# Token mixing whose result is made already transposed: one half of one batch in PSUM, the other half by DMA

## Chip, cores and metric

The kernel runs on one core of a Trainium2 chip. The metric is the device time of one execution in microseconds (us), as the median of several runs. The chip's profiler gives, for one execution, what each engine did: TensorE (PE, with its weight loads as PEld), VectorE (DVE), ScalarE (ACT), GpSimd (POOL) and SyncE (SP), whose queue issues most of the DMAs.

## What is computed

A gated linear recurrence over 768 tokens, in 4 batches with 8 heads of 48, gives x of 768 x 384 for each batch; a token and channel mixer follows.

```python
for t in range(S):                                   # B, H, S, D = 4, 8, 768, 48
    state = alpha[:, :, t, :, None] * state + k_t (outer) v_t
    y[:, :, t] = q_t @ state
x = y as (B, S, H * D)                               # 768 tokens x 384 channels
h = relu(x^T @ w_tok1) @ w_tok2                      # 768 -> 256 -> 768, over the tokens
u = x + h^T
out = u + relu(u @ w_ch1) @ w_ch2                    # 384 -> 1536 -> 384, over the channels
```

Inputs, weights and output are float32; the products are made in bfloat16 with float32 sums.

## The kernel before

**Pieces.** A batch is cut into three attention blocks of 256 tokens, numbered 0 to 11 over the four batches (0, 1, 2 are batch 0's). For each block four loads of 384 KB bring alpha, k, q and v (`ld_at`, `ld_kt`, `ld_qt`, `ld_vt`). ScalarE takes logarithms, TensorE sums them up (`cum`, or `cumw` in batch 0), ScalarE makes the factors `E` and `IE`, VectorE or GpSimd scale k and q by them (`kk`, `qq`; line 700), TensorE or the DMA transposes them (`trk`, `trq`; line 712; `dk`, `dq`; line 725), a copy brings them to SBUF (`evk`, `evq`), TensorE makes the scores (`G0`, `G1`), VectorE masks them (`mask`, line 770), and TensorE makes the state (`K`) and the output (`ia`, `ib`, `y`), which is copied to x (`x0`, `x1`: two tiles of 128 tokens to a block). The state is carried on with one addition and one multiplication (`sa` line 841, `sm` line 844). `vs`, `ka`, `kb` and `kc` are copies that shift halves between partitions.

**Mixer.** `t1_b_m_kc` (line 878) sums x^T @ w_tok1 over the six token tiles, `ht` is its relu (lines 873 and 875). `t2_b_i` (line 883) makes the tile of 128 tokens with number i of h^T, by two products of 384 columns, and `u_b_i` (line 887, VectorE) adds x and writes u in bfloat16. The channel products need u^T. For batch 0 (`UP = (0,)`) TensorE transposes u in 18 products of 128 columns (`up`, line 894), and three copies of 768 columns bring the result to `ut`; for the other batches the DMA transposes u in two halves of three tiles each (`ux`, line 729, issued by SP). `c1_b_mc_half` (line 902) makes hidden columns 128 mc to 128 mc + 127 for the first or the second three token tiles in three products of 384 columns; `rt` is its relu. `c2_b_i_q4` (line 907) sums the second channel product for token tile i in four parts of three products, `o` (line 911, VectorE) adds u, and `st` stores 192 KB. The last token tile to be done, tile 0 of batch 3, is cut into two column halves, `h0` and `h1`.

**Weights.** Each weight piece is loaded as 384 KB of float32 into one of the 19 buffers `in` (`ldw`) and cast into its bfloat16 place (`cw`). A piece of w_ch1 is one of three chunks of 128 input channels by 768 hidden columns; a `c1` waits for three pieces (0, 1, 2 for mc under 6, else 3, 4, 5). A piece of w_tok2 is one of two chunks of 128 rows by all 768 tokens; each `t2` waits for both.

**Order.** The program names every operation in one list, `ORDER`, whose last letter says the engine: t TensorE, s ScalarE, v VectorE, g GpSimd, y SP. Every engine works through its own operations in that order, and waits in it. `BUFS` gives the buffer of each value in the same order. So what runs beside what, and what stands behind a wait, can be read from the list. Operations of VectorE and GpSimd that share a port (`kk`, `qq`, `vb`, `vs`, `ka`, `kb`, `kc`, `sm`, `P`, `k0a`, `q0r`, `pq`, `cw`) wait for each other wherever the list changes from the one engine to the other. `f1_...` to `f12_...` are filler products of 512 columns on zeros: the number is how many such units they are worth, and the rest of the name is the operation ahead of which they stand. PSUM has eight banks; `pair` values take two adjacent ones.

The list of before around the place of the change begins batch 0's mixer with `t1_0_0_0t f1_G0_2t G0_2t`, goes on to

```
t1_0_1_4t x1_2s t1_0_0_4t f1_t1_0_1_5t t1_0_1_5t ht_0_1v P4g cw_wt21s t1_0_0_5t ht_0_0s f3_t2_0_0t t2_0_0t t2_0_1t
```

and, after the token products, has `cum4t trk3t ut_0_0v up_0_2t ut_0_2v ut_0_1s c1_0_11_0t c1_0_8_0t` among the loads and scalings of block 3.

Of the kernel before, what the change touches and what calls it, by code (L numbers as in the profile page):

```python
# [9 lines left out]
BF16 = mybir.dt.bfloat16  # L10
# [84 lines left out]
B, H, S, D = 4, 8, 768, 48  # L95
# [6 lines left out]
UP = (0,)  # L102
# [18 lines left out]
def build(g):  # L121

    P = Plan()
# [6 lines left out]
    def fillers():  # L130
        for o in list(P.ops):
            nm = o.name
            if "PE" in o.eng and (nm[:4] in ("t1_0", "t2_0", "up_0") or nm.split("_")[-1][-1] in "0123" and nm[:2] not in ("t1", "t2", "up", "c1", "c2") and not nm.endswith("10") and not nm.endswith("11")):
# [182 lines left out]
    def mixer(b):  # L316
# [15 lines left out]
        us = []  # L332
        for i in range(NS):
            if i % 3 == 0:
                u = V("u")
            bank = V("one")
            o = P.op(f"t2_{b}_{i}", pe([384] * 2), m0 + (1900 + 330 * i) * sc, writes=[bank],
                     reads=[h for h, _ in hts], preds=[h for _, h in hts] + [wl[("wt2", p)] for p in range(2)],
                     emit=lambda e, i=i, bank=bank: g.tok2(bank, i, [h for h, _ in hts]))
            uo = P.op(f"u_{b}_{i}", dve(384), m0 + (1950 + 330 * i) * sc, writes=[u], reads=[bank, x[i][0]], preds=[o],  # L340
                      emit=lambda e, i=i, bank=bank, u=u: g.uadd(u, i, bank, x[i][0]))
            us.append((u, uo))
        ut = V("ut")
        uts = []
        if b in UP:
            for p in range(3):
                bank = V("one")
                o = P.op(f"up_{b}_{p}", pe([128] * 6), m0 + (3900 + 340 * p) * sc, writes=[bank],
                         reads=list(dict.fromkeys([us[2 * p][0], us[2 * p + 1][0]])),
                         preds=[us[2 * p][1], us[2 * p + 1][1]],  # L350
                         emit=lambda e, p=p, bank=bank: g.utr(bank, [us[2 * p][0], us[2 * p + 1][0]], p))
                uts.append(P.op(f"ut_{b}_{p}", either(dve(768, True), act(768)), m0 + (3950 + 340 * p) * sc, writes=[ut],
                                reads=[bank], preds=[o], emit=lambda e, p=p, bank=bank: g.utev(e, ut, bank, p)))
        else:
            for half in range(2):
                uts.append(P.op(f"ux_{b}_{half}", {"SP": (1240.0, 1240.0)}, m0 + (3900 + 500 * half) * sc, writes=[ut],
                                reads=[us[3 * half][0]], preds=[us[3 * half + i][1] for i in range(3)],
                                emit=lambda e, half=half: g.uxbar(ut, us[3 * half][0], half),
                                dma=("x", 1450.0, 1180.0, 480.0)))
# [13 lines left out]
        for i in range(NS):  # L373
            hold = 4000.0 if (i >= NS - 3 and b < B - 1) else 0.0
            cuts = [(0, HD // 2), (HD // 2, HD)] if (b, i) == LAST else [(0, HD)]
            for ci, (ca, cz) in enumerate(cuts):
# [3 lines left out]
                for q4 in range(4):  # L380
                    pp = []
                    for mc in range(3 * q4, 3 * q4 + 3):
                        pp.append(rts[mc][1][i // 3])
                    prev = P.op(f"c2_{nm}_{q4}", pe([cz - ca] * 3), m0 + (16700 + 1950 * i + 487 * q4) * sc + hold,
                                writes=[bank], reads=[rts[mc][0] for mc in range(3 * q4, 3 * q4 + 3)],
                                preds=pp + [wl[("wc2", mc // 2)] for mc in range(3 * q4, 3 * q4 + 3, 2)] + ([prev] if prev else []),
                                emit=lambda e, i=i, q4=q4, bank=bank, ca=ca, cz=cz: g.ch2(bank, i, q4, rts, ca, cz))
                oo = P.op(f"o_{nm}", dve(cz - ca), m0 + (16750 + 1950 * (i + 1)) * sc + hold, writes=[o_],
                          reads=[bank, us[i][0]], preds=[prev],
                          emit=lambda e, i=i, bank=bank, o_=o_, ca=ca, cz=cz: g.oadd(o_, bank, us[i][0], i, ca, cz))  # L390
# [19 lines left out]
ld_at1y ld_at0y ln1s ln0s f8_cumw1t f1_cumw1t cumw1t IE1s cumw0t IE0s ld_vt0y E0s vb0g vs0_0g vs1_0v ld_kt0y kk0v  # L410
f8_trk0t f1_trk0t trk0t E1s ld_qt0y qq0v ka0s kb0s kc0v f1_trq0t trq0t ld_kt1y kk1v K0t evq0s s0_0v ld_vt1y vb1s
f1_trk1t trk1t ld_at2y evk0v ln2s f2_G0_0t G0_0t ld_qt1y ka1g sa1_0v f4_cumw2t cumw2t mask0_0v vs0_1s kb1g kc1g vs1_1s
K1t sm1_0g qq1v sa0_1v sm0_1v G1_0t ld_kt2y IE2s E2s trq1t evq1s ib0t mask1_0v f3_y1_0t y1_0t y0_0t evk1v G0_1t sa1_1v
ld_qt2y x1_0s mask0_1v G1_1t ld_vt2y x0_0s vb2s kk2g trk2t kc2s ldw_wt10y qq2g cw_wt10s f2_ia1t ia1t mask1_1v evk2s
trq2t ld_at3y vs1_2g ldw_wt11y evq2v ib1t y1_1t y0_1t vs0_2g ldw_wt21y sm1_1g P3g K2t sa0_2v sm0_2g x0_1s t1_0_0_0t
f1_G0_2t G0_2t ldw_wt20y G1_2t cw_wt20g t1_0_1_0t mask0_2v x1_1s t1_0_1_1t ld_at4y ld_kt3y t1_0_1_2t lnP3s cum3t
# [549 lines left out]
```

## Time and profile before

| | before |
|---|---|
| median of 3 runs (lowest, highest) | 163.35 us (163.22, 163.51) |
| span of the profiled execution, from its first to its last instruction | 160.5 us |
| own time of the profiled execution | not on the page; it has the span alone |
| TensorE busy | 154.6 us, 96% of the span |
| VectorE busy | 114.9 us, 72% |
| ScalarE busy | 97.8 us, 61% |
| GpSimd busy | 80.8 us, 50% |
| granted TensorE clock | 1.000 |
| DMA traffic | 35.05 MB, mean 218 GB/s |

A row of the timeline gives start, length, engine, line, operation and the tiles out<-in. A row of groups gives the count, the busy time and the mean duration of one, and the idle time of the engine ahead of them with what ended it. Matmuls are pipelined, so the durations of neighbours overlap; the spacing of a long run of them tells the price of one. "SPq" is SP's queue at the issue of a DMA. A table by stretches gives for each stretch the busy time of each engine, the granted clock, the DMA share and GB/s.

### The profile page before, as it was taken

The numbers are of one execution on the slowest core, as the hardware profiler recorded it, in microseconds if no ns is written. First come the engines' busy times: TensorE is split into PE (matmuls) and PEld (weight loads), VectorE is DVE, ScalarE is ACT, GpSimd is POOL, SyncE is SP. The second block draws the span as 40 slices with busy tenths as digits, with TensorE's granted clock in tenths as the row PEclk, the third lists the DMA queues.
The fourth block names the chain that finished last, engine by engine and source line by source line (L and its number), as shares of the span: only waits on it lengthen the run. The fifth ranks groups of instructions, "written<-read, shape, count | busy, mean of one in ns | idle before, by whom it ended". The sixth has DMA issues, their size and how long they took to land.

```text
span 160.5 us, 3971 instructions
## 1 busy us (share of the span) xinstructions
PE 154.6 (96%) x1563; PEld 97.1 (60%) x1563; DVE 114.9 (72%) x206; ACT 97.8 (61%) x179; POOL 80.8 (50%) x94
## 2 busy tenths in 40 slices
PE   7999989999999999999999999999999999999992
PEld 2545565766667676666667666566567665665661
DVE  6099994979889787989969758795886762464222
ACT  3789999998899955897563583269832203343000
POOL 5205897695973649389778852699523000000000
PEclk9999999999999999999999999999999999999999
DMA  4999999999999999999989999989701235111133
GB/s 122 320 324 317 317 374 311 339 333 306 316 347 324 275 278 272 210 228 319 241 202 298 239 315 204 217 196 134 196 21 62 87 79 169 49 49 53 49 129 116
DMA packets 76130, 35.05 MB, mean 218 GB/s; under 512 B 70352, under 2 KB 74320, under 8 KB 76112
## 3 DMA queue, kind: packets, MB, share of 16 engines
q1 hardware_dynamic: 73808, 31.76, 74.1%
q10 hardware_dynamic: 2304, 3.05, 5.3%
q8 instruction: 12, 0.20, 0.5%
q14 instruction: 6, 0.05, 0.1%
HBM read 25.17 MB, written 4.72 MB: 186 GB/s over the span
## 4 chain that ended last, share of the span: by engine, by line
PE 61%; DMA 12%; DVE 6%; ACT 6%; SPq 6%; POOL 4%; issue 3%; DVEq 0%; POOLq 0%
PE ps L907 22%; PE ps L902 21%; PE ps L643 11%; DMA in<-in_v_dram 6%; SPq L584 6%; DMA out_dram<-o 4%; PE ps L878 3%; PE ps L883 2%; DMA ut<-u 2%; DVE pkk L700 2%; DVE gtm L770 1%; PE ps L712 1%; DVE rt L875 1%; POOL vb L746 1%; POOL pkq L700 1%
## 5 line engine op out<-in xcount | busy, mean ns | idle before, releaser
L907 PE MATMUL ps<-wc,rt 128*128 128x384 bf16 (+1 forms) x300 | 52.4, 319 | 0.0
L902 PE MATMUL ps<-ut,wc 128*128 128x384 bf16 x288 | 50.3, 326 | 0.1
L902 PEld LDWEIGHTS <-wc 128*128 128x128 bf16 x288 | 27.1, 98 | 17.9 <-DMA ut<-u 0.6
L907 PEld LDWEIGHTS <-rt 128*128 128x128 bf16 x300 | 27.8, 98 | 16.0
L873 ACT ACTIVATE rt<-ps 128x384 bf16<-128x384 f32 x47 | 21.4, 492 | 23.6 <-PE ps L902 23.3
L875 DVE TENSOR_SCALAR rt<-ps 128x384 bf16<-128x384 f32 x49 | 25.6, 551 | 9.1 <-PE ps L902 8.9
L770 DVE TENSOR_TENSOR gtm<-ps,mk 128x1024 bf16<-128x1024 f32 x24 | 28.5, 1218 | 3.1 <-PE ps L643 2.8
L911 DVE TENSOR_TENSOR o<-ps,u 128x384 f32<-128x384 f32 (+1 forms) x25 | 13.2, 536 | 12.6 <-PE ps L907 10.1
L700 POOL TENSOR_TENSOR pkk<-in,IE 128x768 bf16<-128x768 f32 x8 | 14.5, 1817 | 3.3 <-DVE ss L844 2.3
L745 ACT CAST x<-ps 128x384 bf16<-128x384 f32 x20 | 9.2, 479 | 11.1 <-PE ps L643 9.5
L887 DVE TENSOR_TENSOR u<-ps,x 128x384 bf16<-128x384 f32 x24 | 12.0, 550 | 3.1 <-PE ps L883 2.5
L746 POOL CAST vb<-in 64x384 bf16<-64x384 f32 (+1 forms) x14 | 8.3, 594 | 10.4 <-DMA in<-in_v_dram 4.7
L692 POOL TENSOR_TENSOR in<-in,in 128x384 f32<-128x384 f32 x8 | 8.0, 1000 | 10.5 <-DVE u L887 3.8
L643 PE MATMUL ps<-rt 128*128 128x512 bf16 (+1 forms) x29 | 12.1, 515 | 1.1 <-DVE rt L541 1.1
L745 ACT CAST vb<-in 64x384 bf16<-64x384 f32 (+1 forms) x18 | 11.4, 634 | 0.8 <-DMA in<-in_v_dram 0.3
L700 POOL TENSOR_TENSOR pkq<-in,E 128x768 bf16<-128x768 f32 x6 | 10.9, 1818 | 0.6 <-DMA tpk<-pkq 0.3
L878 PE MATMUL ps<-x,wt 128*128 128x384 bf16 x48 | 11.0, 325 | 0.0
L844 POOL TENSOR_TENSOR ss<-tmp,E 128x384 bf16<-128x384 f32 x10 | 8.3, 833 | 4.2 <-DVE in L628 3.9
L841 DVE TENSOR_TENSOR tmp<-ps,ss 128x384 f32<-128x384 f32 x16 | 8.8, 552 | 1.8 <-PE ps L643 0.6
L883 PE MATMUL ps<-ht,wt 128*128 128x384 bf16 x48 | 9.1, 326 | 0.0
L643 PE MATMUL ps<-vb,gtm 128*128 128x48 bf16 x192 | 8.2, 183 | 0.2 <-DVE gtm L770 0.2
L643 PE MATMUL ps<-tpq,tpk 48*64 48x128 bf16 (+1 forms) x288 | 7.9, 218 | 0.4 <-POOL tpq L746 0.3
(94 smaller groups left out, 207.6 us busy)
## 6 DMA issues: line engine op xcount, KB each, us to landing
in<-in_alpha_dram SPq DMA_DIRECT2D x12, 384.0 KB, 5.1
in<-in_v_dram SPq DMA_DIRECT2D x12, 384.0 KB, 5.6
in<-in_k_dram SPq DMA_DIRECT2D x12, 384.0 KB, 5.2
in<-in_q_dram SPq DMA_DIRECT2D x12, 384.0 KB, 5.5
in<-in_moe_w_ch_dram SPq DMA_DIRECT2D x12, 384.0 KB, 5.9
out_dram<-o ACTq DMA_DIRECT2D x15, 192.0 KB, 1.8
in<-in_moe_w_tok_dram SPq DMA_DIRECT2D x4, 384.0 KB, 6.0
out_dram<-o SPq DMA_DIRECT2D x8, 192.0 KB, 2.2
```

What stands on the lines that cost most here:

```text
L643: return self.pe.matmul(out, lhsT=lhsT, rhs=rhs, start=start, stop=stop, skip_group_check=True)
L700: self.shared(self.eng[e].tensor_tensor(self.t(dst)[:, :, h0:h1, 0:D], self.t(src)[:, h0:h1].rearrange("p h s d -> p s h d"), bass.AP(tens ...
L745: return self.act.copy(d, s)
L770: self.nc.vector.tensor_tensor(self.t(gtm)[:, hf, :, :], self.pair(gp).rearrange("p a (j t) -> p (a j) t", t=128), bass.AP(tensor=m.tensor ...
L873: self.act.activation(d, s, AF.Relu)
L875: self.nc.vector.tensor_scalar_max(d, s, 0.0)
L878: self.pe.matmul(self.bank(bank)[:, 0:HD], lhsT=self.wt1[:, kc, m * 128 : m * 128 + 128], rhs=self.t(x), start=(kc == 0), stop=(kc == NS - 1))
L883: self.pe.matmul(self.bank(bank)[:, 0:HD], lhsT=self.wt2[:, kc, i * 128 : i * 128 + 128], rhs=self.t(hts[kc]), start=(kc == 0), stop=(kc = ...
L887: self.nc.vector.tensor_tensor(self.t(u)[:, i % 3], self.bank(bank)[:, 0:HD], self.t(x), ALU.add)
L902: self.pe.matmul(self.bank(bank)[:, 0:HD], lhsT=self.wc1[:, kc, mc * 128 : mc * 128 + 128], rhs=self.t(ut)[:, 3 * half : 3 * half + 3, kc, ...
L907: self.pe.matmul(self.bank(bank)[:, 0 : cz - ca], lhsT=self.t(rts[mc][0])[:, i * 128 : i * 128 + 128], rhs=self.wc2[:, mc, ca:cz], start=( ...
L911: self.nc.vector.tensor_tensor(self.t(o)[:, ca:cz], self.bank(bank)[:, 0 : cz - ca], self.t(u)[:, i % 3, ca:cz], ALU.add)
```

## The change

For batch 0 the first three token tiles are no longer made as u and then transposed. For each of three chunks j of 128 channels, `xa` puts x^T of the three tiles into a PSUM bank by three identity products of 128 columns, `tt` adds h for the same chunk and the three tiles by two products of 384 columns, and a copy (`ut_0_0_j`) writes a third of that half of u^T. There is then no u for these tiles: the second channel product adds the residual itself, by three identity products of 128 columns on u^T (`resid`) behind the first part of each of c2_0_0, c2_0_1 and c2_0_2, and `o` for them is a plain copy that ScalarE may make too. Tiles 3 to 5 are made as before, and transposed by the DMA (`ux_0_1`) in place of TensorE.

The weight pieces are cut the other way. A piece of w_ch1 holds all three chunks of input channels for 256 hidden columns, so a `c1` waits for one piece; a piece of w_tok2 holds both chunks of rows for 384 tokens, so the first and the second three tiles wait for one piece each. Each load still brings 384 KB.

`ORDER` and `BUFS` are new from the first entry to the last, with 8 fillers in place of 13.

```diff
-UP = (0,)
+UP = ()
+UDIR = (0,)
...
+        if b in UDIR:
+            ut, us, uts = V("ut"), [], []
+            for half in range(2):
+                evs = []
+                if half in (0,):
+                    for j in range(NM):
+                        bank = V("one")
+                        tx = x[3 * half : 3 * half + 3]
+                        xa = P.op(f"xa_{b}_{half}_{j}", pe([128] * 3), ..., emit=... g.xadd(bank, [v for v, _ in tx], j))
+                        o = P.op(f"tt_{b}_{half}_{j}", pe([384] * 2), ...,
+                                 preds=[h for _, h in hts] + [xa, wl[("wt2", half)]], emit=... g.tok2t(bank, half, j, ...))
+                        evs.append(P.op(f"ut_{b}_{half}_{j}", either(act(384), dve(384)), ..., emit=... g.utev3(e, ut, bank, half, j)))
+                    uts.append(evs)
+                    us += [(ut, evs)] * 3
+                else:
+                    ... t2_0_3 to t2_0_5 and u_0_3 to u_0_5, with preds [wl[("wt2", 1)]] ...
+                    uts.append([P.op(f"ux_{b}_{half}", {"SP": (1240.0, 1240.0)}, ..., emit=... g.uxbar(ut, us[3 * half][0], half))])
...
-                         reads=[ut], preds=(uts[0:2 + half] if b in UP else [uts[half]]) + [wl[("wc1", p)] for p in ((0, 1, 2) if mc < 6 else (3, 4, 5))],
+                         reads=[ut], preds=(uts[half] if b in UDIR else uts[0:2 + half] if b in UP else [uts[half]]) + [wl[("wc1", mc // 2)]],
...
+                    ri = q4 == 0 and b in UDIR and i // 3 in (0,)
-                                emit=... g.ch2(bank, i, q4, rts, ca, cz))
+                                emit=... (g.ch2(bank, i, q4, rts, ca, cz), g.resid(bank, ut, i) if ri else None))
-                oo = P.op(f"o_{nm}", dve(cz - ca), ..., emit=... g.oadd(o_, bank, us[i][0], i, ca, cz))
+                oo = P.op(f"o_{nm}", either(act(384), dve(384)) if ri else dve(cz - ca), ...,
+                          emit=... g.copy(e, g.t(o_), g.bank(bank)[:, 0:HD]) if ri else g.oadd(o_, bank, us[i][0], i, ca, cz))
...
-            self.gated(dma(t, self.w[1][128 * piece : 128 * piece + 128, :]), op)
+            w = self.w[1].rearrange("(c p) m -> p c m", p=128)
+            self.gated(dma(t.rearrange("p (c m) -> p c m", c=2), w[:, :, HD * piece : HD * piece + HD]), op)
         elif nm == "wc1":
-            c, h = piece % 3, piece // 3
-            self.gated(dma(t, self.w[2][128 * c : 128 * c + 128, 768 * h : 768 * h + 768]), op)
+            w = self.w[2].rearrange("(c p) m -> p c m", p=128)
+            self.gated(dma(t.rearrange("p (c m) -> p c m", c=3), w[:, :, 256 * piece : 256 * piece + 256]), op)
...
+    def xadd(self, bank, xs, j):
+        for i, x in enumerate(xs):
+            self.mm(self.bank(bank)[:, i * 128 : i * 128 + 128], self.t(x)[:, j * 128 : j * 128 + 128], self.idn, i == 0, False)
+    def tok2t(self, bank, half, j, hts):
+        for kc in range(NDT):
+            self.mm(self.bank(bank)[:, 0:HD], self.t(hts[kc])[:, j * 128 : j * 128 + 128], self.wt2[:, half, kc, :], False, kc == NDT - 1)
+    def utev3(self, e, ut, bank, half, j):
+        self.copy(e, self.t(ut)[:, 3 * half : 3 * half + 3, j, :], self.bank(bank)[:, 0:HD].rearrange("p (i t) -> p i t", i=3))
+    def resid(self, bank, ut, i):
+        for j in range(NM):
+            self.mm(self.bank(bank)[:, j * 128 : j * 128 + 128], self.t(ut)[:, i, j, :], self.idn, False, False)
```

The new list, cut to the loads and to what the prediction follows:

```
loads and SP: ld_at0 ld_at1 ld_kt0 ld_vt0 ld_qt0 ld_at2 ld_kt1 ld_qt1 ld_vt1 ld_qt2 ld_kt2 ld_vt2 ldw_wc10 ldw_wt10
ldw_wc14 ld_at3 ldw_wt11 ldw_wt21 ldw_wt20 ld_at4 ld_qt3 ldw_wc12 ld_kt3 ldw_wc15 ldw_wc11 ld_qt4 ux_0_1 ldw_wc13 ld_vt3 ...
GpSimd: vs1_0 qq1 vb1 qq2 sm1_0 kk2 sm0_1 vs0_2 kc2 sm1_1 vs1_2 sm0_2 P3 cw_wc10 P4 q0r3 cw_wc12 cw_wc11 ...
VectorE from block 2 on: evk2 x0_0 sa1_1 mask0_2 sa0_2 mask1_2 x1_1 cw_wt21 ht_0_1 ht_0_0 u_0_3 ut_0_0_0 ut_0_0_2 u_0_4 u_0_5 qq3 ...
TensorE from f3_G0_1 on: f3 G0_1 f2 ia1 G1_1 trq2 K1 trk2 f3 G0_2 y0_1 K2 xa_0_0_0 G1_2 t1_0_1_0 t1_0_1_1 ia2 y0_2 t1_0_0_0 t1_0_0_1
t1_0_0_2 ib1 y1_1 ib2 y1_2 t1_0_1_2 t1_0_1_3 t1_0_1_4 t1_0_1_5 t1_0_0_3 t1_0_0_4 t1_0_0_5 xa_0_0_2 cum3 xa_0_0_1 t2_0_3 tt_0_0_0
tt_0_0_2 t2_0_4 tt_0_0_1 t2_0_5 cum4 c1_0_8_0 c1_0_0_0 c1_0_9_0 c1_0_1_0 c1_0_5_0 c1_0_4_0 trq3 trk3 c1_0_10_0 c1_0_11_0 c1_0_2_0
G1_3 c1_0_0_1 c1_0_1_1 c1_0_8_1 c1_0_10_1 c1_0_2_1 trq4 c1_0_3_1 c1_0_7_0 ...
the end: c2_3_5_2t c2_3_5_3t o_3_5v st_3_5y c2_3_0h0_2t c2_3_0h0_3t o_3_0h0v st_3_0h0s
```

More of the change, by code (lines that the diff above doesn't have):

```diff
@@ L331, in mixer @@
             hts.append((ht, ho))
[L332 to L342, printed above, removed]
@@ L882, in tok2 @@
         for kc in range(NDT):
[L883 removed]
+            self.pe.matmul(self.bank(bank)[:, 0:HD], lhsT=self.wt2[:, i // 3, kc, i % 3 * 128 : i % 3 * 128 + 128], rhs=self.t(hts[kc]),
                            start=(kc == 0), stop=(kc == NDT - 1))
```

224 lines of the change are left out of this document (130 added, 94 removed), and 22 rows, old and new, of the table BUFS.

## Prediction

> **What bounds the kernel now.** I read the page first (span and busy shares), then the table by stretches of time, to see from when TensorE is full.
>
> ```profile
> span 160.5 us, 3971 instructions
> PE 154.6 (96%) x1563; PEld 97.1 (60%) x1563; DVE 114.9 (72%) x206; ACT 97.8 (61%) x179; POOL 80.8 (50%) x94
> 15.00:20.00 5.00, 4.61 (x83) 3.22 (x82) 4.81 (x7) 4.50 (x7) 3.16 (x2) 1.00 1.13 317
> 20.00:25.00 5.00, 4.53 (x78) 3.18 (x77) 4.88 (x6) 4.74 (x10) 4.25 (x7) 1.00 1.10 365
> 25.00:30.00 5.00, 4.98 (x38) 2.51 (x36) 2.82 (x6) 4.82 (x11) 4.40 (x4) 1.00 1.00 317
> 50.00:60.00 10.00, 9.97 (x136) 7.05 (x135) 8.45 (x13) 8.07 (x14) 4.00 (x6) 1.00 1.04 282
> 110.00:120.00 10.00, 9.72 (x142) 6.40 (x141) 7.50 (x11) 6.99 (x12) 5.44 (x6) 1.00 0.53 122
> 140.00:150.00 10.00, 10.00 (x64) 6.06 (x63) 4.62 (x9) 3.84 (x9) 0.00 (x0) 1.00 0.16 61
> ```
>
> In the rows of stretches the first number after the length is TensorE's busy time, then weight loads, VectorE, ScalarE, GpSimd, and at the end granted clock (1.00), DMA share and GB/s. From 25 us TensorE is never idle for more than some hundredths of a stretch; the worst one quoted, 110 to 120, loses 0.28 us. Before 25 us VectorE is as full (4.88 of 5), and the DMA share is over 1. So there are two parts: a head of some 25 us set by loads, GpSimd and VectorE, and a body in which time is simply the sum of matmuls. A change can pay only by making the head shorter (counted in matmuls still to do), by taking matmuls away, by fewer stalls in the body, or in the last store.
>
> The chain of waits gives the price of a matmul and the end; "x66" is a run of 66 products, and 10.72 / 66 = 0.1624 us each for 384 columns.
>
> ```profile
> 93.33 5.63 DMA out_dram<-o
> 98.95 3.12 DMA ut<-u
> 133.97 10.72 PE ps L902 x66
> 157.42 0.02 issue
> 157.44 0.36 DVE o L911
> ```
>
> The last product ends at 157.42, so 160.5 - 157.42 = 3.08 us are the last addition, its store and the close. The page does not give the profiled execution's own time, only its span; I take it for a median run, so 163.35 - 160.5 = 2.85 us lie around the span, and every difference below is put on 163.35.
>
> TensorE's own timeline shows what the change touches (start, length, line):
>
> ```profile
> 26.94 0.86 PE L643 MATMUL ps<-rt 128*64 128x384 f32 x2
> 27.73 2.28 PE L883 MATMUL ps<-ht,wt 128*128 128x384 bf16 x12
> 29.85 0.83 PE L894 MATMUL ps<-idn,u 128*128 128x128 bf16 x12
> 30.52 0.33 PE L643 MATMUL ps<-la,u 128*128 128x384 bf16 x1
> 30.81 0.61 PE L712 MATMUL ps<-idn,pkk 128*128 128x128 bf16 x8
> 31.25 0.50 PE L894 MATMUL ps<-idn,u 128*128 128x128 bf16 x6
> 31.76 4.55 PE L902 MATMUL ps<-ut,wc 128*128 128x384 bf16 x27
> ```
>
> The first row is a filler (it reads the zeros in rt); L883 is the second token product, L894 the transposes of u, L902 the first channel product. One 128-column product costs about (0.50 - 0.22) / 5 = 0.056 us, 0.22 being a single one's 219 ns below. Between 27.73 and 31.76 are 4.03 us, and in them 12 x 0.1624 = 1.95 of token products, 18 x 0.056 = 1.0 of transposes, 8 x 0.056 = 0.45 of attention 3's transposes and 0.29 of attention 4's cumulative sum (30.52 to 30.81, one product of 384 columns and five small ones): 3.69. So this place holds only 0.34 us of emptiness, plus the filler before it.
>
> **The change part by part.** TensorE's sum: 18 transposes of 128 columns go; nine identity products of x come in ahead, and nine of u^T in the second channel product. Token products stay 12. Net nothing.
>
> ```profile
> L894 PE MATMUL ps<-idn,u 128*128 128x128 bf16 x18 | 1.3, 219 | 0.0
> L643 PE MATMUL ps<-vb,pkk 128*128 128x96 bf16 x48 | 4.0, 205 | 0.0
> L700 POOL TENSOR_TENSOR pkk<-in,IE 128x768 bf16<-128x768 f32 x8 | 14.5, 1817 | 3.3 <-DVE ss L844 2.3 <-PE ps L643 0.7
> L844 POOL TENSOR_TENSOR ss<-tmp,E 128x384 bf16<-128x384 f32 x10 | 8.3, 833 | 4.2 <-DVE in L628 3.9
> L770 DVE TENSOR_TENSOR gtm<-ps,mk 128x1024 bf16<-128x1024 f32 x24 | 28.5, 1218 | 3.1 <-PE ps L643 2.8
> L746 DVE COPY tpk<-ps 128x1024 bf16<-128x1024 bf16 x3 | 2.0, 679 | 0.0
> L841 DVE TENSOR_TENSOR tmp<-ps,ss 128x384 f32<-128x384 f32 x16 | 8.8, 552 | 1.8 <-PE ps L643 0.6 <-POOL ss L844 0.5
> ```
>
> The Trainium skill (Perfetto Trace Analysis, Optimizing Tensor Performance) asks for true transposes in place of ordinary matmuls, which speaks against the identity products; the two top rows do not bear it out, since an ordinary 96-column product has 205 ns and a 128-column transpose 219.
>
> *The head up to the second token product.* The new order loads batch 0's third block as before, but gives GpSimd five long pieces in a row there: qq1, vb1, qq2, the state of block 0, kk2. The load of q for block 1 is the eighth in both; no buffer holds it up in the new order. These rows give the cadence of loads and their time to landing:
>
> ```profile
> 4.28 1.32 SPq L584 DMA_DIRECT2D in<-in_q_dram  x1
> 11.88 1.14 SPq L584 DMA_DIRECT2D in<-in_q_dram  x1
> 13.07 1.14 SPq L584 DMA_DIRECT2D in<-in_v_dram  x1
> in<-in_q_dram SPq DMA_DIRECT2D x12, 384.0 KB, 5.5
> out_dram<-o SPq DMA_DIRECT2D x8, 192.0 KB, 2.2
> ut<-u SPq DMA_TRANSPOSE x6, 3.0
> out_dram<-o SPq DMA_DIRECT2D x1, 96.0 KB, 1.6
> ```
>
> Loads follow each other at about 1.16 us. The fifth is issued at 4.28, so the eighth at about 7.8, landing 5.4 to 5.5 later: 13.2. Then on GpSimd 1.82 + 0.83 + 1.82 + 0.83 + 1.82 = 7.1 (vb1, a cast, taken like the 833 ns row): 20.3. Transposes of k, about 0.65 with the wait: 21.0. On VectorE then one copy (0.68), two pieces of 0.55, a mask, one of 0.55, a mask: 0.68 + 3 x 0.55 + 2 x 1.22 = 4.77, less some 0.3 since back-to-back pieces overlap (six u additions of 0.55 take 2.88 in a row below): 25.5. The same second mask ends in the profile of before at 23.17 + 2.36:
>
> ```profile
> 23.17 2.36 DVE L770 TENSOR_TENSOR gtm<-ps,mk 128x1024 bf16<-128x1024 f32 x2
> 28.27 2.88 DVE L887 TENSOR_TENSOR u<-ps,x 128x384 bf16<-128x384 f32 x6 [0.83 <-PE ps L883]
> ```
>
> The second mask of before is over at 25.53. So the head is no shorter up to here. In the new order one x copy and a weight cast (cw_wt21, which also waits for P3 on GpSimd, sharing its port) still precede ht_0_1 and ht_0_0, both on VectorE; I get the second token products at 27.9 against 27.73. The removed filler buys nothing by itself: the wait for ht was under it, and cum3 with two xa groups now fills the same gap. Bounds for this step: -0.5 (loads landing a little sooner) to +0.6 (each of five handovers costing a tenth more).
>
> *From there to the first channel product.* 27.9 + 12 x 0.1624 + cum4's 0.29 = 30.14, and the copy of the last u^T group, whose products are the last but one, is over some 0.2 later: first channel product at 30.35 instead of 31.76. But trk3 (0.45) and nine identity products (0.50) have moved behind that point, so the gain in matmuls still to do is 1.41 - 0.45 - 0.50 = 0.46. The three-chunk pieces matter here: a channel product now needs one cast weight piece, and wc10 and wc14 come early enough (thirteenth and fifteenth load), at the price of the token weights coming two places later (nineteenth load issued at about 20.6, landed at 26.0, before it is needed). Bytes per load are the same.
>
> *The transpose of the second half.* It is new on SP's queue behind 26 loads, and issued when u_0_5 is written, about 30.8. Nothing of before shows a transpose that early; the nearest rows are 93.33 and 98.95 above. There a store stood behind a run of loads and took 5.63 where 2.2 is usual, so it sat behind the loads; transposes follow in the same order.
>
> ```profile
> 93.33 3.16 SPq L624 DMA_DIRECT2D out_dram<-o  x2
> 96.97 3.29 SPq L729 DMA_TRANSPOSE ut<-u  x2
> ```
>
> Of the two transposes issued in the 3.29 us from 96.97, the second started at 98.95 and landed 3.12 later; the first, by 1.3 us of spacing, about 1.85 after the backlog had cleared at 98.95. In the new kernel load 26 goes out at about 28.7 and lands near 34.0; the transpose then lands at 35.9. TensorE meanwhile has nine first-half channel products (27 x 0.1624 = 4.39), two groups of attention 3's transposes (0.9) and one score group (0.3): 30.35 + 5.6 = 35.95. It is on time by nothing. Ends: 0 if the queue is shorter, +1.1 if it lands 3.1 after the backlog; I take +0.2. Behind it on SP wait wc13, vt3 and what follows; wc13 would land at about 37.3, is cast by 38.2, and is needed by TensorE at 39.3.
>
> The Trainium skill (Advanced Engine Details and Errata, X-Bar Transpose (TRN2)) calls such transposes as fast as ordinary DMAs, 350-400 GB/s; 295 KB would then be an estimated 0.8 us, the half would be there at 34.8, and the +0.2 would be 0. The 3.12 us row speaks for the slower price.
>
> *VectorE and ScalarE.* Three u additions (0.55), two u^T copies (0.55) and one on ScalarE (0.80) go; three copies of 384 come, and two of three output copies can go to ScalarE. In the body this lies beside TensorE's work: 0.
>
> *The end.* The new order ends o_3_5 (192 KB, SP), then half h0 (96 KB, ScalarE). c2_3_5 ends six half-width products, 0.50 us, before the last. Its store lands 0.02 + 0.55 + 2.2 - 0.50 = 2.27 after the last product (0.55 like the other additions of 384); now the last store lands 0.02 + 0.36 + 1.6 = 1.98 after it. +0.3; at best 0, if the big store takes 1.9.
>
> *Body.* The whole order is new. The stretches quoted show 0.03 and 0.28 us lost; I keep that loss equal, ends -0.4 and +1.0.
>
> Sum: +0.17 is already in the 30.35; -0.46 + 0.2 + 0.3 + 0 = +0.04, so 163.35 + 0.04 = **163.4**. The ends: -0.46 - 0.5 - 0.4 = -1.4 and -0.46 + 0.6 + 1.1 + 0.3 + 1.0 = +2.5.
>
> **The rivals.**
>
> *Head shorter (faster).* If loads land in 5.0 rather than 5.4 us and handovers run as tightly as in the profile, the second token products come 0.5 sooner, the transpose is on time, and the big last store costs nothing: -0.46 - 0.5 = -0.96, 162.4. For: the new order never waits for an input buffer between load 18 and the transpose. Against: VectorE at 4.88 of 5.
>
> *The transpose is late (slower).* It decides from a landing after 36 us. At 3.1 us behind the backlog it lands at 37.1; TensorE stands 1.1 us at c1_0_0_1, as no half-0 work is queued ahead (the next, c1_0_7_0, is seven groups further). With the end's 0.3: -0.46 + 1.1 + 0.3 = +0.9, 164.3. For: the 5.63 us store. Against: the 1.85 us reading.
>
> *Cold TensorE (slower).* Fillers fall from 36 units of 512 columns to 24, and only 3 of the new ones stand after G1_1. These rows are the same seven filler products, first cold, then after work:
>
> ```profile
> 1.06 4.21 PE L643 MATMUL ps<-rt 128*64 128x384 f32 x7 [1.06 <-DVE rt L541]
> 7.34 2.26 PE L643 MATMUL ps<-rt 128*64 128x384 f32 x7
> ```
>
> 4.21 against 2.26 is nearly double. Should TensorE be cold from 21 to 26, the 2.8 us of work there would take 5.6 and some 1.6 of it would show: 165.0. The Trainium skill (TensorE: Matmul & The Clock Gate, Why this matters for your kernels) sets the limit at gaps of about 3 us; I find none so long.
>
> *Banks (slower).* c2_0_1, 3, 2 and 4 stay open together from about 46 to 54.7, holding four of eight PSUM banks while attention 4 and 5 need pairs. If one score group waits for one mask, 1.2 us less an estimated 0.4 of cover: +0.8, 164.2.
>
> **How the numbers follow.** No net change, 162.9 to 163.9: 0.38, of which faster 0.10, within 0.2% 0.17, slower 0.11 (0.2% is 0.33 us, about what a measurement of this kernel tells from no change). Head shorter 0.28, transpose late 0.18, cold 0.10, banks 0.06. So faster 0.10 + 0.28 = 0.38, same 0.17, slower 0.11 + 0.34 = 0.45. Range 162.2 to 164.8: it leaves out the cold case and the far end of the fast one.
>
> **What would show it.** Right: L883-type products starting near 27.9, L902's first near 30.4, no idle of TensorE over 0.3 at the second halves near 36. A weight-load wait of 0.5 or more on the DMA of ut there is the late transpose; single 384-column products longer than 0.2 us apart near 22 to 26, the cold case; waits of score groups on masks near 50, the banks. The first L902 before 29.9 with no such wait would make the forecast too slow; after 31.0, too fast.

## Result and the profile after

The changed kernel takes 171.98 us (median of 4 runs, 171.55 to 173.05); the kernel before, on the same chip in the same session, 163.28 us (4 runs). The ratio is 1.056 with a 95% interval of 1.051 to 1.060. The forecast of 163.4 us, and its range up to 164.8, were wrong. The profiled execution of the changed kernel took 172.22 us by its own time, with a span of 170.5.

The page of the changed kernel has one microsecond more of TensorE work on a span that is ten longer; then its table by stretches (columns as in the prediction):

```profile
span 170.5 us, 3938 instructions
PE 155.6 (91%) x1553; PEld 96.8 (57%) x1553; DVE 111.5 (65%) x197; ACT 100.2 (59%) x189; POOL 77.0 (45%) x90
...
50.00:60.00 10.00, 9.96 (x129) 6.96 (x127) 7.36 (x11) 8.04 (x15) 5.79 (x8) 1.00 1.05 299
60.00:70.00 10.00, 8.59 (x73) 5.28 (x71) 5.20 (x10) 6.49 (x15) 7.24 (x7) 1.00 1.09 262
70.00:80.00 10.00, 9.27 (x75) 5.16 (x76) 6.52 (x11) 6.59 (x13) 3.61 (x5) 0.83 1.05 236
90.00:100.00 10.00, 8.45 (x112) 5.53 (x111) 7.49 (x13) 3.84 (x7) 4.42 (x5) 1.00 1.04 298
100.00:110.00 10.00, 9.53 (x68) 5.64 (x67) 5.45 (x11) 5.17 (x12) 5.54 (x4) 1.00 0.43 100
110.00:120.00 10.00, 7.93 (x82) 4.68 (x81) 7.13 (x11) 7.25 (x17) 5.03 (x5) 1.00 0.96 188
120.00:130.00 10.00, 9.19 (x146) 6.18 (x145) 6.42 (x9) 8.13 (x16) 5.78 (x6) 1.00 0.41 113
140.00:150.00 10.00, 10.00 (x64) 6.05 (x62) 4.36 (x10) 2.93 (x7) 0.00 (x0) 1.00 0.42 118
```

From 25 to 60 us little is wrong (TensorE is idle for 0.97 us, against 0.12 in the kernel before), and from 130 us nothing. Between 60 and 120 us it stands idle for 1.41 + 0.73 + 1.55 + 0.47 + 2.07 = 6.2 us, where the kernel before lost 0.35, then for another 0.81 up to 130 us, and in one stretch its clock is 0.83. Most of the loss is in the body, not at the place of the change.

Its timeline on TensorE, at the head and at batch 1's first channel product:

```profile
27.56 0.48 PE L922 MATMUL ps<-ht,wt 128*128 128x384 bf16 x2
...
30.00 3.08 PE L957 MATMUL ps<-ut,wc 128*128 128x384 bf16 x18
...
34.02 0.62 PE L751 MATMUL ps<-idn,pkk 128*128 128x128 bf16 x8 [0.49 <-DVE pkk L739]
...
70.73 7.71 PE L957 MATMUL ps<-ut,wc 128*128 128x384 bf16 x36 [2.14 <-DMA ut<-u]
...
97.26 0.32 PE L917 MATMUL ps<-x,wt 128*128 128x384 bf16 x1 [1.55 <-DVE o L966]
```

The second token products (L922) start at 27.56 and the first channel product (L957) at 30.00, both a little sooner than forecast. The first long wait stands at 70.73: 2.14 us for the DMA transpose of batch 1's u. The 36 products behind it take 7.71 us, 0.214 each, against 0.162 for a run at full speed: 36 x (0.214 - 0.162) = 1.9 us more that the busy time doesn't show.

SP's queue just ahead of that wait, then the chain of waits over the same time and further on:

```profile
60.92 2.14 SPq L621 DMA_DIRECT2D in<-in_q_dram  x1
63.16 1.58 SPq L621 DMA_DIRECT2D in<-in_alpha_dram  x1
65.02 2.71 SPq L768 DMA_TRANSPOSE ut<-u  x1
67.83 1.70 SPq L764 DMA_TRANSPOSE tpk<-pkq  x1
69.63 1.27 SPq L768 DMA_TRANSPOSE ut<-u  x1
```

```profile
65.02 5.66 DMA ut<-u
...
70.73 7.71 PE ps L957 x36
...
91.68 4.88 DMA out_dram<-o
...
96.65 0.57 DVE o L966
...
97.26 0.32 PE ps L917
```

The transpose goes out at 65.02 right behind a run of loads, and its issue alone takes 2.71 us; it lands 5.66 us after its start, where the median before was 3.0. In the kernel before the last load ahead of the same transpose is issued at 59.29, and the transpose at 64.68, in 1.29 us:

```profile
59.29 1.61 SPq L584 DMA_DIRECT2D in<-in_v_dram  x1
...
64.68 1.29 SPq L729 DMA_TRANSPOSE ut<-u  x1
```

So the transpose starts at nearly the same time in both; what is late is its landing. The second part of the chain is a store: 4.88 us for 192 KB. VectorE's addition at 96.65 waits for it, because it needs the store's output buffer, and TensorE's product at 97.26 waits for that addition.

The waits by releaser and the DMA issues say how often:

```profile
DVE o L966 <- DMA out_dram<-o: 8.6, 4, 3.8
DVE o L785 <- DMA out_dram<-o: 2.1, 1, 2.1
ACT o L784 <- DMA out_dram<-o: 1.6, 1, 1.6
```

```profile
out_dram<-o ACTq DMA_DIRECT2D x16, 192.0 KB, 3.8
...
ut<-u SPq DMA_TRANSPOSE x7, 4.1
```

The same two views of the kernel before:

```profile
DVE o L911 <- DMA out_dram<-o: 2.5, 3, 1.6
```

```profile
out_dram<-o ACTq DMA_DIRECT2D x15, 192.0 KB, 1.8
```

VectorE and ScalarE stood 8.6 + 2.1 + 1.6 = 12.3 us for stores (2.5 us in the kernel before), and the median store on ScalarE's queue took 3.8 us where it took 1.8. The Trainium skill (DMA: Bandwidth & Descriptors, Queues, rings and completion order) says that the DMA engines take turns between the queues packet by packet; the 4.88 us of a store on another queue, in a stretch with 298 GB/s of traffic, fit that, though no run here tests it.

### The profile page after: what moved, and what is told of

The parts are those of the page before. It is cut to its first block, busy times and chain, and to the rows that moved or that the text cites. A ratio compares the mean times of both kernels' runs of the same rounds, so it can differ in the third digit from the quotient of the medians.

```text
span 170.5 us, 3938 instructions
## 1 busy us (share of the span) xinstructions
PE 155.6 (91%) x1553; PEld 96.8 (57%) x1553; DVE 111.5 (65%) x197; ACT 100.2 (59%) x189; POOL 77.0 (45%) x90
## 4 chain that ended last, share of the span: by engine, by line
PE 50%; DMA 15%; POOL 10%; DVE 9%; issue 6%; SPq 6%; ACT 2%; POOLq 0%; DVEq 0%; ACTq 0%
PE ps L962 18%; PE ps L957 17%; PE ps L682 9%; DMA in<-in_k_dram 4%; DMA ut<-u 3%; DMA out_dram<-o 3%; DMA tpk<-pkq 3%; SPq L643 3%; PE ps L917 2%; DVE pkk L739 2%; POOL pkq L739 2%; PE ps L922 2%; DMA in<-in_moe_w_ch_dram 2%; POOL pkk L739 2%; POOL tpq L785 2%
## 5 line engine op out<-in xcount | busy, mean ns | idle before, releaser
L957 PE MATMUL ps<-ut,wc 128*128 128x384 bf16 x288 | 52.3, 333 | 4.3 <-DMA ut<-u 2.6
L957 PEld LDWEIGHTS <-wc 128*128 128x128 bf16 x288 | 27.7, 100 | 23.8 <-DMA ut<-u 3.9
L912 ACT ACTIVATE rt<-ps 128x384 bf16<-128x384 f32 x58 | 26.3, 491 | 23.2 <-PE ps L957 22.7
L914 DVE TENSOR_SCALAR rt<-ps 128x384 bf16<-128x384 f32 x38 | 19.5, 550 | 13.7 <-PE ps L957 13.7
L966 DVE TENSOR_TENSOR o<-ps,u 128x384 f32<-128x384 f32 (+1 forms) x22 | 11.6, 536 | 14.6 <-DMA out_dram<-o 8.6
L883 POOL TENSOR_TENSOR ss<-tmp,E 128x384 bf16<-128x384 f32 x14 | 11.7, 836 | 15.9 <-DVE tmp L880 15.6
L784 ACT CAST x<-ps 128x384 bf16<-128x384 f32 x15 | 7.1, 478 | 15.1 <-PE ps L682 15.0
L667 POOL TENSOR_TENSOR in<-in 128x384 f32<-128x384 f32 x8 | 8.0, 1000 | 3.6 <-DVE pkq L739 1.6
L682 PE MATMUL ps<-rt 128*64 128x384 f32 (+1 forms) x19 | 8.5, 562 | 1.1 <-DVE rt L578 1.1
L682 PEld LDWEIGHTS <-tpk 48*64 48x64 bf16 (+1 forms) x288 | 5.9, 102 | 6.0 <-issue 3.8
L739 DVE TENSOR_TENSOR pkq<-in,E 128x768 bf16<-128x768 f32 x8 | 7.6, 953 | 1.3 <-POOL wc L785 1.0
L922 PE MATMUL ps<-ht,wt 128*128 128x384 bf16 x42 | 8.4, 326 | 0.0
```

Of the source, the lines that this page charges most:

```text
L682: return self.pe.matmul(out, lhsT=lhsT, rhs=rhs, start=start, stop=stop, skip_group_check=True)
L739: self.shared(self.eng[e].tensor_tensor(self.t(dst)[:, :, h0:h1, 0:D], self.t(src)[:, h0:h1].rearrange("p h s d -> p s h d"), bass.AP(tens ...
L784: return self.act.copy(d, s)
L883: self.shared(self.eng[e].tensor_tensor(self.st(self.t(s)), self.st(self.t(t)), self.amul(E, hf, wide), ALU.mult))
L912: self.act.activation(d, s, AF.Relu)
L914: self.nc.vector.tensor_scalar_max(d, s, 0.0)
```

## The experiments

Three candidates for the lost time had to be told apart: the place of the transposes behind loads on SP, the stores with three output buffers, and the change proper (a DMA transpose more among the first batch's loads). An edit of `ORDER` is given by the operations that move; buffers were given anew where needed. Each group of runs was compared with runs of the kernel before on its own chip; these lie between 162.41 and 163.60 us, and each ratio uses its own. A gain of one version over another is a difference of medians from two chips; by the ratios it can come out up to 0.9 us different. Spans and times differ by about 1.7 us.

**A splice, an order edit, six output buffers, the pieces alone.**

```diff
 e1  ORDER: the changed list up to rt_0_7_1 (about 44 us), then the operations that are left, in the order of the kernel before
 e2  ORDER: ... ux_1_0y ld_at9y ld_qt8y ...      (both loads were ahead of ux_1_0); ln19, r19 behind rt_1_10_1
-e3  "rt": 20, "o": 3
+e3  "rt": 17, "o": 6
 e4  the kernel before with its own ORDER; only the cut of the w_ch1 and w_tok2 pieces is the new one
```

> The changed kernel's list up to the last relu of batch 0's first channel product, and from there on the list of before (its remaining operations in its own order). Theory A (the loss is in the new list behind batch 0: transposes of u and stores stand behind prefetch loads, and output additions wait for stores): the head's gain stays and the rest runs as before, 162.0 to 163.6 us. Theory B (the parts of the change itself cost: identity products, residual, more work on ScalarE and fewer fillers): 168 us or more, like the changed kernel.

Measured 166.16 us (165.36 to 166.89; ratio 1.023, 1.018 to 1.028), between the two expectations. Its stretches:

```profile
45.00:50.00 5.00, 3.94 (x54) 2.55 (x54) 3.04 (x7) 4.53 (x9) 3.12 (x4) 1.00 1.04 298
50.00:60.00 10.00, 9.06 (x111) 6.05 (x106) 8.10 (x11) 7.36 (x12) 4.76 (x7) 1.00 1.05 302
60.00:70.00 10.00, 10.00 (x103) 6.64 (x101) 8.26 (x15) 5.95 (x14) 6.19 (x6) 1.00 1.05 259
```

With the old order behind 44 us TensorE is full from 60 us on, but for 0.55 us at 110 to 120, so some 5.8 us of the 171.98 belong to the new list from there. The largest part of what is left is lost at the seam, 1.06 + 0.94 us between 45 and 60, where ScalarE and GpSimd wait for weights and v that land late.

> The changed kernel with two loads (alpha of block 9, q of block 8) taken from ahead of batch 1's first transpose of u to right behind it, and the two ScalarE operations that read the first of them a few places later. Theory A: the transpose lands some 2 us sooner, TensorE's idle stretch of 2.1 us near 70 us falls under 0.5 us, the slow clock after it goes, and the time falls by 2 to 4 us, to 168 to 170. Theory B, or theory C (the transpose's own length, not the queue, is what TensorE waited for): no change within 0.5 us.

Measured 174.89 us (ratio 1.075): a miss, slower than the changed kernel. The wait at batch 1's first half is gone: its transpose leaves at 65.25, no sooner than the 65.02 of the changed kernel, but lands 3.1 us later in place of 5.66. But the two loads now stand ahead of its second half, and the wait is there, with the slow clock behind it (18 products in 4.78 us, 0.266 each):

```profile
74.62 4.78 PE L957 MATMUL ps<-ut,wc 128*128 128x384 bf16 x18 [2.87 <-DMA ut<-u]
```

> The changed kernel with six output buffers in place of three (and 17 relu buffers in place of 20, to make room). Theory A: the 10 us that VectorE waits for stores go, the stalls of TensorE near 97 and 112 to 115 us with them, and the time falls by 2 to 5 us, to 167 to 170. Theory B: the waits go but the time stays within 0.7 us, as VectorE is off the path.

Measured 167.96 us (167.13 to 168.63; ratio 1.034): 4.0 us of the loss, as theory A had it, without a step of the order changed. No wait for a store is left among the waits that the view lists; the waits for transposes are, shorter:

```profile
69.55 6.02 PE L957 MATMUL ps<-ut,wc 128*128 128x384 bf16 x36 [0.82 <-DMA ut<-u]
```

> The kernel before with only the weight pieces cut the new way, its list and buffers untouched. Theory A: 163.3 us, within 0.4. Theory D (rows of 1 and 1.5 KB in place of 3 KB make the weight loads slower, and the head and the body late): over 164.5 us.

Measured 163.86 us (10 runs, 162.12 to 165.23; ratio 1.004, 1.000 to 1.008). That is just above theory A's range (163.7) and far below theory D's: the cut of the pieces costs at most 0.8%, or 1.3 us, and perhaps nothing.

**The late splice, and loads moved.** e5 keeps the changed list up to about 60 us; e5b is e5 with six output buffers; e6 moves transposes in the changed list; e7 is the converse, in the kernel before.

```diff
 e5  ORDER: the changed list up to ld_at7 and what is issued with it; then the old order; ld_kt8 behind ux_1_0; u_1_4, c2_0_5 and the last outputs of batch 0 a few places moved
 e6  e3, and ORDER: ... ux_1_0y ux_1_1y ld_at9y ld_qt8y ... dq6y ...; ux_2_1 ahead of dq9
 e7  the kernel before, and ORDER: ... ld_at9y ld_vt7y ld_qt8y ld_at10y ux_1_0y ...
```

> The kernel before with one thing changed: four prefetch loads (alpha 9, v 7, q 8, alpha 10) moved ahead of batch 1's first transpose of u on SP, with buffers that are free. Theory A: the transpose lands 3 to 6 us later than it is needed, TensorE stands for it and then runs at half rate for a few us: 166 to 170, with a wait on the DMA of ut of over 1.5 us near 68. Theory B (the queue's order does not matter, the new order's matmul and VectorE order does): 162.9 to 164.3.

Measured 170.19 us (169.73 to 170.69; ratio 1.046, 1.043 to 1.050), 0.2 above the range of theory A. This one edit makes the old kernel as slow as the new one nearly is. SP's queue and TensorE's timeline:

```profile
64.44 0.57 SPq L584 DMA_DIRECT2D in<-in_alpha_dram  x1
...
66.92 1.17 SPq L584 DMA_DIRECT2D in<-in_alpha_dram  x1
68.19 2.59 SPq L729 DMA_TRANSPOSE ut<-u  x1
```

```profile
73.67 4.98 PE L902 MATMUL ps<-ut,wc 128*128 128x384 bf16 x15 [5.54 <-DMA ut<-u]
```

The transpose leaves 3.5 us later than the 64.68 of before, lands 5.4 us after its issue, TensorE stands 5.54 us, and 15 products then take 0.332 us each, half speed, 15 x 0.17 = 2.5 us more. 5.54 + 2.5 = 8.0, against 168.4 - 160.5 = 7.9 us of span. So loads ahead of that transpose are shown to make such a wait, with its price, in a kernel that has nothing of the change. Here four loads also delay the start, which the changed kernel's do not.

> The changed kernel's order is kept up to its last loads before batch 1's first transpose of u (about 60 us, past the second token products' first half of batch 1); from there the order of the kernel before runs, with two weight-free loads fewer ahead of that transpose. Theory A (the loss comes from what stands ahead of batch 1's and 2's transposes and stores on the DMA queues in the new order's body): the head's gain of 0.5 to 0.8 us stays, the waits at 68 and 100 to 120 us go: 162.3 to 163.6. Theory B (the head's part of the new order hands on a debt of loads or of VectorE's work whatever the body is): 166 or more.

> The same late splice with six output buffers for three (paid for by three of the 20 relu buffers). Theory A: with the old order's body no store holds up the output copies that TensorE waits for, so within 0.4 us of the splice alone: 162.0 to 163.6. Theory B: the three output buffers are a bound of their own and it gains over 1 us on the splice alone.

Measured 172.38 (ratio 1.059) and 170.47 us (1.045): by the numbers theory B. The profiles say why, and it is neither theory: the seam itself. In e5 TensorE waits 5.67 us for a relu of VectorE, which stands behind an output copy that waits 5.48 us for a store; in e5b the store is out of the way and the same relu stands 3.57 us behind a GpSimd step that waits 7.58 us for the load of k 8, which the splice had moved. Six buffers gain 1.9 us here.

```profile
78.04 1.12 PE L957 MATMUL ps<-ut,wc 128*128 128x384 bf16 x3 [5.67 <-DVE rt L914]
```

> The changed kernel with six output buffers, and on SP both transposes of batch 1's u ahead of the two prefetch loads (alpha 9, q 8) and of the attention transpose dq6, and batch 2's second one ahead of its load and dq9. Theory A (the place in the queue makes the wait): of the 167.96 of six outputs alone the waits of 0.82 and 1.06 us and what follows them go: 165.5 to 167.2, and no wait of TensorE on the DMA of ut over 0.5 us. Theory B (the DMA engines are full and the transposes take long in any place): 167.6 or more, with the waits still there.

Measured 173.76 us (ratio 1.067), a miss for both theories. TensorE's wait on u's transposes near 70 is gone, and dq6, pushed back behind the two loads, makes a longer one. ScalarE's timeline, where the copy of q stands ahead of the relus, and TensorE's:

```profile
76.89 1.33 ACT L784 COPY tpq<-tpk 128x1024 bf16<-128x1024 bf16 x1 [5.89 <-DMA tpk<-pkq]
```

```profile
79.40 2.08 PE L957 MATMUL ps<-ut,wc 128*128 128x384 bf16 x6 [5.01 <-ACT E L715]
```

**The transposes themselves.** e8 makes batch 0's second half in PSUM too, so no DMA transpose is left there; e8b is e8 with six output buffers; e9 adds one to the kernel before; e10 moves the two loads behind four transposes.

```diff
-e8  if half in (0,):                 i // 3 in (0,)
+e8  if half in (0, 1):               i // 3 in (0, 1)      ORDER: xa_0_1_j, tt_0_1_j, ut_0_1_j for t2_0_3 to 5, u_0_3 to 5; no ux_0_1
+e9  P.op("uxd", SP, writes=[a free ut buffer], reads=[u of tiles 3 to 5]), behind ld_vt3 in the old ORDER
 e10 e3, and ORDER: ux_1_0 dq6 ux_1_1 dk6 ld_at9 ld_qt8; ln19, r19, q0r8, qq8 later
```

> The kernel before with one DMA transpose of half of batch 0's u added on SP behind its 27th load (about 31 us), into a buffer that nobody reads; nothing else changes. Theory S: every later load lands 2 to 3.5 us later, and as the loads are full to 61 us and attention and weights wait on them, 164.5 to 168. Theory L (a transpose among the loads is hidden): 162.5 to 163.8.

Measured 164.88 us (164.32 to 165.05; ratio 1.011, 1.004 to 1.018): theory S, at its lower end. The added transpose is issued at 31.06, holds SP's queue for 4.36 us and lands 8.2 us after its issue. The stretch from 35 us in the kernel before, then three of this run:

```profile
35.00:40.00 5.00, 5.00 (x45) 3.17 (x44) 4.80 (x10) 4.34 (x8) 3.16 (x5) 1.00 1.10 313
```


```profile
35.00:40.00 5.00, 5.00 (x44) 2.98 (x43) 4.70 (x10) 4.84 (x8) 2.81 (x5) 1.00 1.12 222
40.00:45.00 5.00, 5.00 (x46) 3.15 (x46) 3.28 (x4) 3.32 (x7) 4.46 (x4) 1.00 0.99 301
45.00:50.00 5.00, 3.26 (x47) 2.43 (x46) 3.77 (x7) 3.88 (x7) 3.29 (x5) 1.00 1.11 336
```

While the transpose runs the DMA share is 1.12, as full as ever, but only 222 GB/s move; the kernel before moves 313 in that stretch. Counting the loads issued on SP's queue up to 40 us gives 36 in the kernel before, 31 here, and 32 in the changed kernel. TensorE pays at 45 to 50 us, with 1.74 us idle: it waits for VectorE, which stands behind GpSimd steps that had waited 1.47 us for a load of alpha, and ScalarE's casts wait 0.90 + 1.07 us for weights. The kernel before has none of these waits for loads. So a transpose that nobody waits for costs about 2 us (2.5 by the medians and spans, 1.8 by the ratio, whose interval is 0.7 to 2.9), by what it takes out of a run of loads that lasts until about 61 us.

> The changed kernel, but batch 0's second half of u is made transposed in PSUM as well, with its residual by identity products: the DMA transpose ux_0_1 is gone from SP's queue, 18 products of 128 columns (about 1.0 us) come to TensorE, the rest of the list stays. Theory S (the load stream is a second bound: DMA is full from 10 to 65 us, and the transpose at 30.5 us takes some 3 us out of it, so that five loads fewer are out by 40 us and batch 1's first transpose meets the end of the stream): the stream ends earlier, the wait of 2.14 us at 70.7 and the half rate behind it shrink or go, 165 to 169 in spite of the products added. Theory L (the order of the list is to blame, whatever the DMA transpose takes): 171.5 to 174.

> The same with six output buffers. Theory S: against the 167.96 of six outputs alone it pays 1.0 us of products and saves the waits at 69.5 us and their aftermath: 165.5 to 168. Theory L: 168.5 to 170.

Measured 173.74 (ratio 1.065) and 172.06 us (1.053): theory L by the number for e8, above both theories for e8b; the runs don't decide. The wait at batch 1's first transpose is gone in both (TensorE is full from 65 to 80 us), yet the new copies in VectorE's list make other waits, of relus, masks and scalings among them, between 30 and 50 us, 4.7 us in e8, so TensorE comes later as well as the loads sooner.

> The changed kernel with six output buffers, and the prefetch loads alpha 9 and q 8 behind all four transposes of that place (both of u, q and k of attention 6), with the work that reads them moved behind too. If two loads ahead of the transposes make the wait that is left at 69.5 us: 166.2 to 167.4, and no wait of TensorE on the DMA of ut near 70 us. If a load stream that ends too late makes it whatever these two do: 167.5 to 169.

Measured 174.47 us (ratio 1.068), neither theory. Its profiled execution was 3.9 us longer than the median, so only the places are read: the wait on u's transpose is down to 0.17 us, and a wait of 5.37 us for a relu of VectorE stands at 88.61 instead, where the work that reads the moved loads now is.

**Mended seam, and a control.**

```diff
 e11 e5b, and ORDER: ux_1_0 ahead of dk6; ld_kt8 behind ux_1_1, its reader k0a8 just ahead of kk8; o_0_5, st_0_5 behind rt_1_4_0
-e12 the kernel before, "rt": 20, "o": 3
+e12 "rt": 17, "o": 6
```

> The late splice with six output buffers, mended at its seam: both transposes of batch 1's u now leave ahead of the attention transpose dk6 and of the load of k 8, and the GpSimd step that reads that load is moved behind, where nothing waits for it. Theory A (the seam's in-order waits made the 170.47, not the head): the 3.57 us wait at 75 us and the half rate behind it go, 163 to 165.5, with TensorE full from 60 to 120 us. Theory B (the head's part hands a debt on): over 167, the wait moving to yet another place.

Measured 166.85 us (165.45 to 167.91; ratio 1.025, 1.016 to 1.035), between the expectations: the 3.57 us wait and the slow clock are gone, smaller waits at the seam stay (60 to 80 us lose 1.05 + 1.86 us), and behind them TensorE is full:

```profile
60.00:70.00 10.00, 8.95 (x67) 5.50 (x66) 5.09 (x11) 6.06 (x14) 4.63 (x4) 1.00 0.84 225
70.00:80.00 10.00, 8.14 (x82) 4.75 (x81) 7.43 (x14) 6.78 (x13) 8.93 (x8) 1.00 1.01 263
80.00:90.00 10.00, 10.00 (x118) 6.42 (x116) 8.44 (x16) 6.31 (x14) 7.42 (x8) 1.00 1.06 218
```

> The kernel before with six output buffers for three, the same edit that took 4.0 us off the changed kernel. Theory A (three output buffers bind only where stores stand behind loads, which the old order avoids): 162.0 to 163.4, no change that can be told. Theory B (three output buffers bind in any order): 161.5 or less.

Measured 162.97 us against 163.60 (10 and 13 runs; ratio 0.998, 0.994 to 1.003): no change. Three output buffers are a bound that can be told only together with the new order of stores and loads.

**Bytes taken away, nothing moved.** Since each reordering made a new wait, the last two runs leave the order alone.

```diff
+e13 the changed kernel; in load(): if op.name in ("ld_qt7", "ld_qt8"): h1 = 1
+e14 e3, and the same for ld_qt7, ld_qt8, ld_qt11, ld_kt10, ld_kt11
```

> The changed kernel in its own order, with two of the loads ahead of batch 1's first transpose of u (q 7 and q 8) cut to one head of eight, 48 KB for 384; the rest of q 7 and q 8 is left out, so blocks 7 and 8 work on old data. Nothing is moved, so no other wait is made. Theory A (the loads ahead of that transpose make the wait of 2.14 us at 70.7 and the half rate behind it, some 1.8 us): both go, 166.5 to 169. Theory B (the wait comes from DMA traffic as a whole, or moves on to the next operand whatever stands there): 170 or more.

Measured 169.18 us (168.62 to 169.66; ratio 1.039, 1.035 to 1.044): 2.8 us less than the changed kernel, 0.2 above the range of theory A. Its stretches:

```profile
60.00:70.00 10.00, 10.00 (x92) 6.36 (x89) 6.48 (x13) 7.64 (x17) 7.64 (x7) 1.00 0.89 236
70.00:80.00 10.00, 9.95 (x103) 6.03 (x101) 9.07 (x16) 7.32 (x17) 6.92 (x7) 1.00 1.07 216
```

The transpose now lands in time, TensorE is full from 60 to 80 us and the clock stays at 1.00. SP's queue, then a wait on TensorE that the changed kernel's profile hasn't:

```profile
65.61 1.34 SPq L770 DMA_TRANSPOSE ut<-u  x1
```

```profile
31.17 0.32 PE L684 MATMUL ps<-la,u 128*128 128x384 bf16 x1 [1.50 <-ACT la L675]
```

The transpose leaves even later than the 65.02 of the changed kernel, and lands 3.1 us after its issue in place of 5.66: the loads ahead of it set how long it takes. The cut also takes 0.67 MB out of the stream; that the place alone can do it is shown by e2 and e7, which only move loads. With a wait of 1.50 us for alpha standing ahead in this profile, the 2.8 us may be too small for this place, where 2.14 + 1.9 us were lost. The waits for stores are still there (VectorE's output addition waits 9.2 us for them).

> The changed kernel with six output buffers, and five loads cut to 48 KB in the same way: q 7 and q 8 ahead of batch 1's first transpose, q 11, k 10 and k 11 around batch 2's. Most of those blocks' q and k is left out. Theory A: of the 167.96 of six outputs alone the wait of 0.82 us near 69.5, the 1.06 near 109 and most of the 1.48 near 116 go: 164.0 to 166.0. Theory B: 167 or more.

Measured 166.51 us (164.88 to 167.28; ratio 1.020, 1.013 to 1.026): 1.45 us below six buffers alone, 0.5 above the expected range. The waits of 0.82 and 1.06 us are gone; one of 1.54 for a transposed q at 116 us stays, and its profile shows 1.58 us at 32 us, for a load of alpha, like e13's.

## Why the prediction was wrong

**Head, right.** Second token products at 27.56 (forecast 27.9), first channel product at 30.00 (30.35): the cadence of loads, the handovers and the matmuls counted between them held to 0.35 us. (The load of q for block 1 is the eighth in the new list, but the ninth in the kernel before, not "the eighth in both"; no term hangs on it.) Two things were not in the sum: a wait of 0.49 us at 34.02 for kk3, and a head that is not always so quick. In three of the 13 profiles with this head (e10, e13, e14) TensorE stands 1.5 to 1.75 us for alpha of block 4, and the first channel product comes at 31.5 to 32.6.

**Transpose of batch 0's second half, right as far as it was costed.** It was issued at 30.52 and landed 5.8 us later, at 36.3 (forecast 35.9); the products that need it start at 36.42 without a wait (the sum had +0.2, by the slower price). The rule of the Trainium skill (Advanced Engine Details and Errata, X-Bar Transpose (TRN2)) that such a transpose is as fast as a copy gave 0 there too; but the fall from 313 to 222 GB/s in e9 at a full DMA share speaks against it. The 5.66 us of batch 1's doesn't by itself, since the loads issued just ahead of it took 5.5 to 6.7 us to land. What the step left out is the other side: "Behind it on SP wait wc13, vt3 and what follows" looked at the next few loads, where the price, about 2 us in the old order (e9), comes out 5 to 10 us after the landing.

**TensorE's sum, right.** The identity products cost what the transposes did: three of them at 48.14 take 0.33 us, (0.33 - 0.22) / 2 = 0.055 us each against 0.056.

**The end, right.** Its last product ends at 167.19, the span at 170.5: 3.3 us against 3.08, +0.2 for a forecast of +0.3.

**The base, off by 1.1 us, without effect.** 2.85 us were put around the span by taking the profiled execution of before for a median one. Executions with the span of 160.5 took about 162.2 us, so 1.7 us lie around it, and the profiled one of before was a quick one. All differences stay; but the ten us between the two spans are 8.7 us between the medians.

**The body, wrong: the step that failed.** "I keep that loss equal, ends -0.4 and +1.0." The whole list had been reordered, and no row was asked what each queue holds ahead of batch 1's and 2's transposes and stores. That loss is most of the +8.7 us. Of it the runs show: stores that come back late to three output buffers, 4.0 us (e3; nothing that can be told in the old order, e12); the loads ahead of batch 1's first transpose, 2.8 us (e13; 7.4 in the converse, e7); both fixes and the three other small loads together take 5.5 (e14), so the two are not simply added. A DMA transpose among the loads costs about 2 us in the old order (e9); that it is the same amount in the new one was not shown, as e8 doesn't decide. The cut of the pieces is at most 1.3 us of it (e4). What makes up the 2% (some 3 us) that are left between e14 and the kernel before is not settled beyond its waits at 32 and 116 us.

**The rivals.** Two had the right mechanism and the wrong place. "The transpose is late" was priced for ux_0_1 at 36 us, at 1.1; it was ux_1_0 at 70.7, at 2.14. "Cold TensorE" was looked for where fillers had gone, from 21 to 26 us; it came behind that wait, at 1.9 us for 1.6 priced. Banks and a shorter head played no part that shows. A rival on the new list's later batches was missing, though the profile of before showed its price: a store of 5.63 us behind loads stands in the prediction's own rows.

No version beat the kernel before; e1 and e11, which have the changed head and the old body, stay 3.4 and 3.3 us above it, for the most part by their seams (2.0 and 2.9 us of TensorE idle).

## What to carry to other kernels

A schedule in fixed lists is tuned as a whole: when a change brings a new list, read for each DMA that TensorE or an output buffer waits for what stands ahead of it on its queue, in every batch, before calling the body neutral. Moving transfers, alone or by a splice, moved the wait to another waiter five times here (e2, e5, e5b, e6, e10); to learn whether a transfer is the cause, take its bytes away and leave the order alone. A transfer that nobody waits for is not free when the load stream is full: cost what it takes out of the stream, and look for the payer later (here some 10 us).

## What the runs showed of the hardware

A wait of 2.14 us was enough to put TensorE at half rate: over 70 to 75 us the granted clock is 0.66. The Trainium skill (TensorE: Matmul & The Clock Gate, Why this matters for your kernels), with its limit of about 3 us, would have left it at full speed; the measurement decides. After 0.82 us (e3) it stayed full. Between them the length of the gap doesn't decide it: the same 15 products behind the same two waits of 1.11 and 1.45 us ran at full speed in e8 and at 0.276 us each in e8b (TensorE's timelines):

```profile
39.77 2.60 PE L958 MATMUL ps<-ut,wc 128*128 128x384 bf16 x15 [1.45 <-DVE gtm L810]
```

```profile
39.08 4.14 PE L958 MATMUL ps<-ut,wc 128*128 128x384 bf16 x15 [1.45 <-DVE gtm L810]
```

And a DMA transpose of half a u right behind a run of loads holds SP's queue for 2.6 to 4.4 us (2.59 in e7, 4.36 in e9), against 1.29 in the kernel before, where the last load had been issued at 59.29, and 1.34 in e13.
